# Where tiles begin in SBUF: weights, x and g moved to multiples of 256 bytes in an attention and ReLU-squared feed-forward kernel

## The chip, the cores and the metric

The kernel runs on one core of a Trainium2 chip. The metric is the device time in microseconds of one execution; several executions are timed, and one is profiled.

## The reference

Block-diagonal attention (chunks of 64 positions, no mask), then a feed-forward layer with a squared ReLU, all in float32:

```python
batch, n_heads, seq, head_dim = (8, 8, 576, 64)      # q, k, v
n_tokens, d_model, d_ff = (4608, 512, 2048)          # w_in, w_out

scores = scale * np.matmul(q_c, k_c.transpose(0, 1, 2, 4, 3))   # per chunk of 64
scores = scores - np.max(scores, axis=-1, keepdims=True)
attn = np.exp(scores)
attn = attn / (np.sum(attn, axis=-1, keepdims=True) + 1e-09)
out = np.matmul(attn, v_c)
...
x = out.transpose(0, 2, 1, 3).reshape(B * S, H * D)
h = x @ w_in
r = np.maximum(h, 0.0)
g = r * r
return (g @ w_out).astype(np.float32)
```

The weights arrive as 64-bit floats and are handed to the kernel as pairs of 32-bit words.

## The kernel before

The 4608 tokens are 36 pairs of chunks (128 tokens each), in 9 blocks of 4 pairs. A block's attention output is kept transposed as `xh` and `xl`, a high part in fp32r and the rest, so that a product of float32 quality comes from three fp32r matmuls (high by high, high by low, low by high). The feed-forward part walks over 9 blocks x 16 slices of 128 hidden units. In a slice, L514 makes `h` (128 hidden units x 512 tokens) from 4 x 3 matmuls, in which a piece of `wi` is the resident operand and x moves. ScalarE and VectorE make g = relu(h) squared and split it into `gh` and `gl` (L525 to L541). Two slices later L551 adds 4 x 3 matmuls into four accumulators `o`; there gh or gl is resident and `wo` moves. So each of the 144 slices has 24 matmuls of 128x128 by 512 columns, 3456 in all, each with a weight load of its own.

In the first 120 us the weights come in: `fetch_w` (L126) loads a slice of 64-bit words, and `convert_w` (L137) turns them into float32 and splits them into a high and a low part with ScalarE and VectorE (L147 to L186). Beside that the attention of the first 8 pairs runs. The attention of the other 28 pairs (class `Quad`, L262) is spread between the groups of the feed-forward matmuls, from about 125 to 805 us. TensorE is kept warm in the beginning by matmuls of `ident` with itself (L741, L370).

The order of the instructions on each engine comes from a planner (class `Plan`), which gets a cost in microseconds, the names read and the names written for each step and runs a list schedule; addresses play no part in it.

SBUF is given out by pools in the order in which they are opened: `const` (ident, warm, and 32 slots of 4096 bytes per partition for the weights, some of which hold raw q, k, v first), `att` (row maxima and sums, four buffers of 32 bytes), `xp` (x of two blocks), `gp` (g, gh, gl and the output's staging tile ob), `raw`, `wst`, and `nat`, whose room `late` takes over. Within a pool, tiles follow each other in the order of their first use and take multiples of 32 bytes. Before, the first bytes per partition are:

| tile | begins at | beyond a multiple of 256 |
|---|---|---|
| ident | 16512 | 128 |
| warm | 17024 | 128 |
| first slot of the weights | 17056 | 160 |
| row maxima and sums | 148128 | 160, 192, 224, 0 |
| xh of even blocks | 148256 | 32 |
| g | 181024 | 32 |
| ob | 191264 | 32 |
| raw q and k of the later pairs | 195360 | 32 |
| nat, late | 205600 | 32 |

All tiles in and behind the weights' slots are multiples of 2048 bytes, but for the row maxima and sums, so the rest given for the first of a pool holds for all of it.

Of the kernel before, what the change touches and what calls it, by code (L numbers as in the profile page):

```python
# [10 lines left out]
F32 = mybir.dt.float32  # L11
# [9 lines left out]
def kernel(  # L21
# [24 lines left out]
    P = 128  # L46
# [27 lines left out]
    const = ctx.enter_context(tc.tile_pool(name="const", bufs=1))  # L74
    att = ctx.enter_context(tc.tile_pool(name="att", bufs=1))
# [4 lines left out]
        x: ctx.enter_context(tc.tile_pool(name=f"ps_{x}", bufs=1, space=bass.MemoryType.PSUM))  # L80
        for x in ("o", "h", "at")
    }
    turn_at = itertools.count()

    both = psum["at"].tile([P, 2, DM], F32, name="both", tag="both")
# [4 lines left out]
    early = ctx.enter_context(ExitStack())  # L90

    ident = const.tile([P, P], F32, name="ident")
    warm = const.tile([P, 1], F32, name="warm")


    nat = early.enter_context(tc.tile_pool(name="nat", bufs=1))
# [920 lines left out]
```

## Time and profile before

| | |
|---|---|
| runs | 911.04 us, median of 3 (909.97 to 911.22) |
| profiled execution | 911.28 us, of which the span from the first to the last instruction is 909.5 us |
| mean granted clock of TensorE | 0.997 |
| TensorE matmul, weight load, VectorE, ScalarE busy | 897.6, 724.9, 427.1, 329.9 us |
| HBM read, written | 45.09 MB, 9.44 MB |

In the rows of the profile, PE is TensorE's matmul side and PEld its weight loads, DVE is VectorE, ACT ScalarE, POOL GpSimd and SP the engine that issues most DMAs. A group's row gives the line, the engine, the operation, `out<-in` by tile names, the shape, the count, then busy time in us and the mean of one in ns, then the engine's idle time just before them and what ended it. A row of the chain in order of time or of the timeline begins with the start and the length in us. A row of a tile's view gives the least, median and greatest duration in ns. A row of waits gives microseconds in total, times, and the longest.

### The profile page before, as it was taken

To read this page: it belongs to the slowest core of one execution; us is meant where nothing else is said; L and a number is where in the kernel's file an instruction comes from. 1 tells how busy PE (TensorE), PEld (TensorE's weight loads), DVE (VectorE), ACT (ScalarE), POOL (GpSimd) and SP (SyncE) were. 2 spreads that over 40 slices of the span, in tenths; PEclk is the share of its full clock that TensorE was granted. 3 is DMA by queue.
4 is the path that set the end of the run, shared out by engine and by line. 5 is a ranking of instruction groups with operands and counts; after the bars stand their busy time and mean duration, and the time that the engine had idled before them with its cause. 6 is when DMAs were issued, how large, how long until landed. Compare 5 with 4: busy or idle time off the path is not lost.

```text
span 909.5 us, 14995 instructions
## 1 busy us (share of the span) xinstructions
PE 897.6 (99%) x6046; PEld 724.9 (80%) x6046; DVE 427.1 (47%) x746; ACT 329.9 (36%) x565; POOL 6.1 (1%) x12
## 2 busy tenths in 40 slices
PE   8899999999999999999999999999999999999998
PEld 7677777888888888888888888888888888878886
DVE  5999992333444445444443343444444443223222
ACT  4798873334322223222322222223222322222221
POOL 2000000000000000000000000000000000000000
PEclk9999999999999999999999999999999999999999
DMA  9876533222222223111311131123222210001001
GB/s 196 261 210 177 168 65 97 36 48 46 70 48 36 35 35 83 32 33 31 79 33 32 33 81 29 33 35 81 36 36 36 51 42 1 1 1 47 1 1 46
DMA packets 193237, 55.52 MB, mean 61 GB/s; under 512 B 178192, under 2 KB 186640, under 8 KB 193168
## 3 DMA queue, kind: packets, MB, share of 16 engines
q1 hardware_dynamic: 190912, 53.91, 25.7%
q8 instruction: 47, 0.77, 0.4%
q10 hardware_dynamic: 2256, 0.66, 0.3%
q14 instruction: 22, 0.18, 0.1%
HBM read 45.09 MB, written 9.44 MB: 60 GB/s over the span
## 4 chain that ended last, share of the span: by engine, by line
PE 90%; DVE 5%; ACT 3%; issue 1%; POOL 0%; POOLq 0%; ACTq 0%; DVEq 0%
PE h L514 41%; PE o L551 41%; PE both L331 2%; PE both L291 1%; PE pt L321 1%; DVE gl L541 1%; PE both L741 1%; DVE wia L172 0%; ACT qbd L413 0%; DVE wi L186 0%; DVE wia L165 0%; DVE woa L165 0%; PE sc L425 0%; ACT wi L177 0%; DVE woa L172 0%
## 5 line engine op out<-in xcount | busy, mean ns | idle before, releaser
L514 PE MATMUL h<-xh,wi 128*128 128x512 f32 x1152 | 393.4, 398 | 0.1
L551 PE MATMUL o<-wo,gh 128*128 128x512 f32 x1152 | 361.7, 395 | 0.4 <-ACT ob L565 0.4
L514 PEld LDWEIGHTS h<-xh,wi 128*128 128x128 f32 x1152 | 216.1, 188 | 52.2 <-DVE wi L186 0.5
L551 PEld LDWEIGHTS o<-wo,gh 128*128 128x128 f32 x1152 | 215.8, 188 | 50.8 <-ACT ob L565 0.9
L551 PE MATMUL o<-wo,gl 128*128 128x512 f32 x576 | 227.0, 394 | 0.0
L514 PE MATMUL h<-xl,wi 128*128 128x512 f32 x576 | 226.0, 393 | 0.0
L541 DVE TENSOR_TENSOR gl<-g,gh 128x512 fp32r<-128x512 f32 x144 | 99.3, 690 | 207.3 <-ACT gh L538 204.2
L538 ACT CAST gh<-g 128x512 fp32r<-128x512 f32 x144 | 89.4, 621 | 225.7 <-PE o L551 188.4
L525 ACT ACTIVATE g<-h 128x512 f32<-128x512 f32 x144 | 85.6, 594 | 228.8 <-PE h L514 226.5
L529 DVE TENSOR_TENSOR g<-g 128x512 f32<-128x512 f32 x112 | 76.4, 682 | 184.9 <-ACT g L525 184.9
L551 PEld LDWEIGHTS o<-wo,gl 128*128 128x128 f32 x576 | 108.1, 188 | 25.7
L514 PEld LDWEIGHTS h<-xl,wi 128*128 128x128 f32 x576 | 108.5, 188 | 24.0
L297 DVE TENSOR_REDUCE m<-both 128x8 f32<-128x512 f32 x28 | 19.3, 691 | 55.9 <-ACT xh L341 51.8
L307 ACT ACTIVATE e<-e 128x512 f32<-128x512 f32 x28 | 17.7, 632 | 49.6 <-DVE e L301 49.6
L327 ACT COPY p<-pt 128x512 f32<-128x512 f32 x28 | 16.4, 585 | 20.4 <-PE pt L321 20.4
L341 ACT CAST xh<-both 128x512 fp32r<-128x512 f32 x28 | 16.4, 587 | 14.4 <-PE both L291 13.4
L531 ACT ACTIVATE g<-g 128x512 f32<-128x512 f32 x32 | 20.3, 635 | 0.6
L343 DVE TENSOR_TENSOR xl<-both,xh 128x512 fp32r<-128x512 f32 x28 | 19.1, 681 | 2.1 <-ACT xh L341 2.1
L277 DVE STREAM_TRANSPOSE qt<-q_raw 128x512 f32<-128x512 f32 x28 | 19.6, 700 | 0.0
L331 PEld LDWEIGHTS both<-p,v_raw 64*64 64x64 f32 x896 | 15.6, 134 | 4.9 <-issue 4.9
L331 PE MATMUL both<-p,v_raw 64*64 64x64 f32 x896 | 19.4, 224 | 0.0
L316 DVE TENSOR_TENSOR e<-e,z 128x512 f32<-128x512 f32 x28 | 19.2, 685 | 0.1
(85 smaller groups left out, 461.6 us busy)
## 6 DMA issues: line engine op xcount, KB each, us to landing
wiraw<-in_moe_w_in_dram SPq DMA_DIRECT2D x16, 512.0 KB, 6.6
woraw<-in_moe_w_out_dram SPq DMA_DIRECT2D x16, 512.0 KB, 5.8
out_dram<-ob SPq DMA_DIRECT2D x32, 256.0 KB, 2.0
q_raw<-in_q_dram SPq DMA_DIRECT2D x224, 32.0 KB, 2.2
k_raw<-in_k_dram SPq DMA_DIRECT2D x224, 32.0 KB, 2.2
v_raw<-in_v_dram SPq DMA_DIRECT2D x56, 128.0 KB, 3.3
vbd<-in_v_dram SPq DMA_DIRECT2D x32, 64.0 KB, 3.3
qk_raw<-in_q_dram SPq DMA_DIRECT2D x14, 128.0 KB, 4.8
```

The lines of the kernel that those rows point to most:

```text
L277: nc.vector.transpose(t.rearrange("p h i -> p (h i)"), pairs[self.pair][nm].rearrange("p h a d -> p (h a d)"))
L297: nc.vector.tensor_reduce(self.m, four[:, :, 0], axis=AX.X, op=ALU.max)
L316: nc.vector.tensor_tensor(self.e, self.e, self.z.broadcast_to([P, HH, 2, CH]), op=ALU.mult)
L331: nc.tensor.matmul(four[to, c, 1, h2], self.v[own, 2 * h2 + w], self.p[own, h2, w], start=True, stop=True)
L343: nc.vector.tensor_tensor(xl, four[:, :, 1], xh.bitcast(F32), op=ALU.subtract)
L514: nc.tensor.matmul(self.h[:, :self.n], a[:, c], bb[:, c, :self.n], start=c == 0 and i == 0, stop=last,)
L525: nc.scalar.activation(self.g, self.h[:, :self.n], AF.Relu)
L529: nc.vector.tensor_tensor(self.g, self.g, self.g, op=ALU.mult)
L531: nc.scalar.activation(self.g, self.g, AF.Square)
L538: nc.scalar.copy(self.gh[:, :self.n], self.g)
L541: nc.vector.tensor_tensor(self.gl[:, :self.n], self.g, self.gh.bitcast(F32)[:, :self.n], op=ALU.subtract)
L551: nc.tensor.matmul(acc[b, j], a[:, j * P:(j + 1) * P], bb, start=f == 0 and i == 0, stop=f == NF - 1 and i == 2,)
```

## The change

An unused tile of 128 bytes per partition is put into `att`, and the tile `warm`, of which one column is used, gets 32 columns (128 bytes) in place of one. Nothing else is edited.

```diff
@@ -80,6 +80,7 @@
         x: ctx.enter_context(tc.tile_pool(name=f"ps_{x}", bufs=1, space=bass.MemoryType.PSUM))
         for x in ("o", "h", "at")
     }
+    att.tile([P, 32], F32, name="edge")
     turn_at = itertools.count()
 
     both = psum["at"].tile([P, 2, DM], F32, name="both", tag="both")
@@ -90,7 +91,7 @@
     early = ctx.enter_context(ExitStack())
 
     ident = const.tile([P, P], F32, name="ident")
-    warm = const.tile([P, 1], F32, name="warm")
+    warm = const.tile([P, 32], F32, name="warm")[:, :1]
 
 
     nat = early.enter_context(tc.tile_pool(name="nat", bufs=1))
```

## Prediction, made before the changed kernel ran

> **What bounds the kernel now.** I read the page's head, then its chain that ended last, then the stages, then who waits for whom.
>
> ```profile
> span 909.5 us, 14995 instructions
> PE 897.6 (99%) x6046; PEld 724.9 (80%) x6046; DVE 427.1 (47%) x746; ACT 329.9 (36%) x565; POOL 6.1 (1%) x12
> ...
> PE 90%; DVE 5%; ACT 3%; issue 1%; POOL 0%; POOLq 0%; ACTq 0%; DVEq 0%
> ...
> L514 PE MATMUL h<-xh,wi 128*128 128x512 f32 x1152 | 393.4, 398 | 0.1
> L551 PE MATMUL o<-wo,gh 128*128 128x512 f32 x1152 | 361.7, 395 | 0.4 <-ACT ob L565 0.4
> ...
> L551 PE MATMUL o<-wo,gl 128*128 128x512 f32 x576 | 227.0, 394 | 0.0
> L514 PE MATMUL h<-xl,wi 128*128 128x512 f32 x576 | 226.0, 393 | 0.0
> ```
>
> The last four lines are the 3456 matmuls of the feed-forward part: two lines of 1152 and two of 576. TensorE is 90% of the chain and, before these lines, it waits for somebody for half a microsecond in all. The mean of 393 to 398 ns is the time that one is in flight; they overlap. What one really costs is read from the chain in order of time, where twelve of them stand together.
>
> ```profile
> 265.69 2.78 PE h L514 x12
> ...
> 777.83 2.78 PE o L551 x12
> ...
> 844.11 2.80 PE h L514 x12
> 846.91 2.80 PE o L551 x12
> ```
>
> So one costs 2.78/12 = 231.7 ns in the middle and 2.80/12 = 233.3 ns towards the end, and 3456 of them about 3456 x 0.232 = 802 us of the span of 909.5. The two lines read quite different operands (x moving against a resident w; w moving against a resident g) and cost the same. Next the stages: busy time of each engine, its count, the granted clock and the DMA share.
>
> ```profile
> 0.00:10.00 10.00, 8.65 (x72) 6.93 (x73) 1.54 (x3) 2.07 (x3) 6.05 (x12) 1.00 0.98 180
> 10.00:60.00 50.00, 45.99 (x474) 37.23 (x474) 48.18 (x96) 40.51 (x74) 0.00 (x0) 0.97 0.88 238
> 60.00:120.00 60.00, 57.72 (x438) 45.12 (x433) 57.49 (x113) 50.72 (x92) 0.00 (x0) 1.00 0.56 167
> 120.00:230.00 110.00, 109.58 (x717) 87.89 (x719) 48.98 (x89) 48.17 (x82) 0.00 (x0) 1.00 0.28 53
> 230.00:800.00 570.00, 570.00 (x3880) 463.16 (x3881) 242.50 (x408) 163.48 (x274) 0.00 (x0) 1.00 0.20 42
> 800.00:910.00 110.00, 105.65 (x482) 84.56 (x480) 28.36 (x41) 24.91 (x42) 0.00 (x0) 0.99 0.05 20
> ```
>
> The columns after the length are PE, PEld, DVE, ACT, POOL. In the first 10 us the DMA engines are full (0.98); from 10 to 120 us VectorE is (48.18 of 50, then 57.49 of 60: it converts weights); from 120 us on TensorE is, without a gap from 230 to 800. Three limits in turn, and an address can touch each of them in another way.
>
> **What the change does.** It adds no instruction and takes none away: one tile that nothing writes or reads (128 bytes in each partition), and 128 bytes in place of 32 for `warm`. In the program's address map of before, ident begins at 16512 and ends at 17024, warm takes 32 bytes, and the weights' slots begin at 17056 = 66 x 256 + 160. There are 32 slots of 4096 bytes, then four 32-byte buffers of `att` up to 148256 = 579 x 256 + 32, where x begins; x, g, ob, the raw tiles and the tiles of the attention are multiples of 2048 bytes behind it. So before, each weight begins 160 beyond a multiple of 256 and everything from x on 32 beyond one. Afterwards warm ends at 17152 = 67 x 256, and `att` at 17152 + 131072 + 256 = 148480 = 580 x 256: the weights move up by 96 bytes, all behind them by 224. That it does what it says is therefore settled, except for ident, which stays at 128 beyond. The planner that orders the instructions knows costs and names, not addresses, so the order on every queue stays. There is no new wait, and nothing is moved past anything. What is left is the price of an address, engine by engine.
>
> **TensorE.** Is a moving operand that begins on a multiple of 64 cheaper than one that begins 32 beyond? The one operand of that kind before is ident, at 16512 = 258 x 64. It moves in the transposes and in the warming matmuls; the whole of a run of them and one's time in flight:
>
> ```profile
> 301.34 0.60 PE L321 MATMUL pt<-ident,e 128*128 128x128 f32 x4
> ...
> 32.43 1.05 PE L370 MATMUL h<-ident 128*128 128x256 bf16 x8
> ...
> L321 PE MATMUL pt<-ident,e x112: 270/272/273, 159.4 to 781.5; 128*128 128x128 f32 x112
> ...
> L370 PE MATMUL h<-ident x8: 272/273/283, 32.4 to 33.2; 128*128 128x256 bf16 x8
> ```
>
> Eight bf16 matmuls of 256 columns start within 1.05 - 0.27 = 0.78 us, so one takes 0.78/7 = 111 ns, or 222 ns for 512 columns. The float32 transposes cost (0.60 - 0.27)/3 = 109 ns for 128 columns. So with an operand on a multiple of 64, 512 columns of bf16 stand at 222 ns and 512 columns of the kernel's type, not on one, at 231.7. The 10 ns between them are the most that I can lay at the door of the address: an estimate of 3456 x 9.7 ns = 34 us, 877 us, is the far end below. But the two rows differ in type as well, and the weight loads say that the type alone does such things:
>
> ```profile
> L321 PEld LDWEIGHTS pt<-ident,e x112: 138/141/142, 159.2 to 781.4; 128*128 128x128 f32 x112
> ...
> L551 PEld LDWEIGHTS o<-wo,gh x1152: 186/188/193, 43.1 to 904.8; 128*128 128x128 f32 x192
> ```
>
> e and gh both begin 32 beyond a multiple of 256, both loads have 128 columns of 4 bytes, and one takes 141 ns and the other 188. The kernel's own type (fp32r) costs 47 ns more with the same alignment. That is the nearest row to the question, and by it I put the 10 ns down to the type too and cost the change at nothing on TensorE. The far end above: 2.78 becomes 2.80 wherever it stands, (2.80 - 2.78)/12 = 1.7 ns for each matmul.
>
> **VectorE and ScalarE.** If wide operands off the boundary cost them a piece more, it would show as a rate below one column per step.
>
> ```profile
> L565 ACT COPY ob<-o 128x512 f32<-128x512 f32 x16 | 9.4, 585 | 4.5 <-DMA out_dram<-ob 3.8
> ...
> L565 ACT COPY ob_last<-o 128x256 f32<-128x256 f32 x2 | 0.6, 375 | 0.8 <-PE o L551 0.8
> ...
> L297 DVE TENSOR_REDUCE m<-both 128x8 f32<-128x512 f32 x28 | 19.3, 691 | 55.9 <-ACT xh L341 51.8
> ...
> L529 DVE TENSOR_TENSOR g<-g 128x512 f32<-128x512 f32 x112 | 76.4, 682 | 184.9 <-ACT g L525 184.9
> ```
>
> ScalarE pays (585 - 375)/256 = 0.82 ns a column, with a fixed part of 585 - 420 = 165 ns. VectorE takes 691 ns where it reads 512 columns of PSUM, which the change does not move, and writes 8, and 682 ns where it reads and writes 512 columns of an SBUF tile that begins 32 beyond. The unaligned access is the quicker by 9 ns. So nothing is to be had there: 0. From 120 us on it would be hidden anyway, since VectorE is busy 242.5 of 570 us.
>
> **The DMAs.** Who waits for them:
>
> ```profile
> DVE ob L565 <- DMA out_dram<-ob: 6.3, 8, 2.1
> ...
> ACT kt L417 <- DMA qk_raw<-in_k_dram: 5.4, 1, 5.4
> ...
> ACT ob L565 <- DMA out_dram<-ob: 3.8, 7, 2.1
> ...
> PE o L551 <- ACT ob L565: 0.4, 1, 0.4
> ```
>
> The stores hold up evictions for 10.1 us in all, and of that 0.4 us comes through to TensorE. The one wait for a load is ScalarE's in the first 8 us. After that the loads run ahead of VectorE, whose whole idle time from 10 to 120 us is 110 - 48.2 - 57.5 = 4.3 us: no quicker load can give more than those 4.3 us plus a few tenths ahead of 10 us. On the other side 0: a descriptor that crosses fewer boundaries has no reason to be slower. I take 0, since VectorE keeps its 105.7 us of work in that stage whatever lands sooner.
>
> The page "DMA: Bandwidth & Descriptors" of the Trainium skill says, in "How a descriptor splits into AXI transactions", that a transaction must start at a multiple of 256 bytes, and that the bytes below an unaligned start are fetched and cost beats. It speaks for a gain here. By it a stored row of 2048 bytes, 32 beyond, would take 9 transactions and 65 beats in place of 8 and 64: an estimate of 1.6% of a store, 0.03 us of the 2.0 us in the row below, once at the end of the kernel. No view of this trace shows a transaction.
>
> ```profile
> out_dram<-ob SPq DMA_DIRECT2D x32, 256.0 KB, 2.0
> ```
>
> **The sum** is 0 + 0 + 0 against the profiled execution's 911.28 us (span 909.5 and 1.8 around it); the median of the three runs is 911.04, 0.24 below it, and their spread 909.97 to 911.22 is 0.14%. I predict 911.0. A shift under 0.2%, 1.8 us, can't be told from none.
>
> **The rivals.**
>
> 1. *TensorE reads an aligned row quicker.* For it: the 10 ns over the bf16 rate that nothing else in the trace explains for certain. Against it: the type differs too, and costs 47 ns in the loads at equal alignment. The time: any value down to 877; each nanosecond is 3.5 us.
> 2. *The start gets shorter* (loads that no longer straddle a boundary, or VectorE). For it: a DMA share of 0.98, then 0.88, in the first 60 us. Against it: VectorE is the limit from 10 us on, and its rate shows no loss. At most 911.0 - 4.3 = 906.7.
> 3. *Slower: TensorE falls into the other rhythm.* Without the attention's matmuls between them (844 us) groups take 2.80, with them 2.78, though code, shapes and alignment are the same; so the spacing hangs on something finer than the instructions. Now w and x both begin at 0 within 256 bytes, in place of 160 and 32, and both are read at once. Were that enough for 2.80 everywhere, its place is the stage from 230 to 800 us:
>
> ```profile
> 230.00:800.00 570.00, 287.03 (x1144) 213.34 (x1145) 1.00 0.20 42
> ...
> 230.00:800.00 570.00, 279.77 (x1140) 214.37 (x1140) 1.00 0.20 42
> ```
>
> (first L514, then L551 alone): 2284 matmuls x 1.7 ns = 3.8 us, 914.8. It decides when half of them change. The other way about, 2.78 throughout, gives the 887 or so matmuls after 120 us and outside this stage 1.5 us, which stays within 0.2%.
>
> **How the numbers follow.** No change: 0.60. Rival 1: 0.18, with a third of it at gains under 9 us. Rival 2: 0.07, of which 0.01 stays within 0.2%. Rival 3: 0.15, of which 0.01 stays within it and 0.04 lies beyond 916, should the two reads cost each other more than the other rhythm does. So faster 0.18 + 0.06 = 0.24, same 0.60 + 0.02 = 0.62, slower 0.14. The range of 902 to 916 holds the forecast, rivals 2 and 3 and the small end of rival 1: 0.60 + 0.07 + 0.11 + 0.06 = 0.84.
>
> **What would show it.** Right: twelve matmuls at 2.78 in the middle and 2.80 at the end, LDWEIGHTS of gh at 188 ns, L529 at 682, L538 at its old duration, the loads' landing times unchanged, and VectorE at 48 of 50 us from 10 to 60. Rival 1: groups of twelve below 2.75 us, all through. Rival 2: the same groups, but the first matmul of L514 earlier and a lower DMA share ahead of 60 us. Rival 3: 2.80 from 230 to 800. I am wrong if the price of a matmul hangs on where its rows begin; since 802 us are made of them, nothing else here could move the time by a per cent.

## The result: 911.04 us becomes 894.43 us, and nearly all of it is in the feed-forward matmuls

The changed kernel takes 894.43 us (median of four, 893.91 to 895.09) against 911.04 us (909.97 to 911.22). The ratio is 0.982, with a 95% interval of 0.9803 to 0.9837: 16.6 us, or 1.8%, faster. It lies below the range forecast, and the likeliest case, no change, did not come about.

The changed kernel's lines are one number higher than before's (L515 is L514, L552 is L551). First the head of its page, two of the four lines of the feed-forward matmuls and the one VectorE line that the forecast named:

```profile
span 893.3 us, 14995 instructions
PE 880.5 (99%) x6046; PEld 724.0 (81%) x6046; DVE 427.1 (48%) x746; ACT 330.4 (37%) x565; POOL 6.1 (1%) x12
...
L515 PE MATMUL h<-xh,wi 128*128 128x512 f32 x1152 | 388.1, 394 | 0.2
L552 PE MATMUL o<-wo,gh 128*128 128x512 f32 x1152 | 356.1, 390 | 0.5 <-ACT ob L566 0.5
...
L530 DVE TENSOR_TENSOR g<-g 128x512 f32<-128x512 f32 x112 | 76.4, 682 | 176.1 <-ACT g L526 176.1
```

The instructions are as many as before on each engine. VectorE is busy 427.1 us both times and L530 takes 682 ns as it did; ScalarE's busy time moves by 0.5 us. TensorE's matmul side is 17.1 us less busy, and its weight loads are not (724.0 against 724.9). The chain in order of time gives the price:

```profile
265.15 2.72 PE o L552 x12
...
840.53 2.72 PE h L515 x12
843.25 2.72 PE o L552 x12
```

Twelve take 2.72 us on both lines, in the middle and near the end: 226.7 ns each, against 231.7 and 233.3 before. The two rhythms of before are gone too. When this builds up is read from the first instruction that takes h out of PSUM in a slice: the first slice and the last from the view of the tile g, the sixteenth after it from the timeline; before, then the changed kernel.

```profile
L525 ACT ACTIVATE g<-h x144: 575/597/612, 36.3 to 897.3; 128x512 f32<-128x512 f32 x144
...
140.75 0.60 ACT L525 ACTIVATE g<-h 128x512 f32<-128x512 f32 x1 [2.35 <-PE h L514]
```

```profile
L526 ACT ACTIVATE g<-h x144: 577/598/605, 35.8 to 881.4; 128x512 f32<-128x512 f32 x144
...
139.97 0.60 ACT L526 ACTIVATE g<-h 128x512 f32<-128x512 f32 x1 [2.27 <-PE h L515]
```

The lead is 0.5 us at the first slice, 0.8 at the seventeenth and 15.9 at the last. Between the first two VectorE is the limit, and cheaper matmuls wait for it. In the 127 slices after that, 15.1 us come from 127 x 24 = 3048 matmuls: 5.0 ns each, the difference that the chain shows. So rival 1 is what happened, at about half its far end. But its mechanism, an aligned row that is cheaper to read, is not what the runs below show.

### The profile page after: what moved, and what is told of

It is laid out like the page before. It is cut to its first block, busy times and chain, and to the rows that moved or that the text cites. A ratio compares the mean times of both kernels' runs of the same rounds, so it can differ in the third digit from the quotient of the medians.

```text
span 893.3 us, 14995 instructions
## 1 busy us (share of the span) xinstructions
PE 880.5 (99%) x6046; PEld 724.0 (81%) x6046; DVE 427.1 (48%) x746; ACT 330.4 (37%) x565; POOL 6.1 (1%) x12
## 4 chain that ended last, share of the span: by engine, by line
PE 88%; DVE 5%; DMA 2%; ACT 2%; issue 1%; SPq 1%; POOL 0%; DVEq 0%; POOLq 0%; ACTq 0%
PE h L515 40%; PE o L552 40%; PE both L332 2%; PE both L292 2%; PE pt L322 1%; DMA k_raw<-in_k_dram 1%; DMA woraw<-in_moe_w_out_dram 1%; DMA qk_raw<-in_k_dram 1%; DVE woa L166 1%; PE both L742 1%; PE sc L426 1%; DVE wi L187 1%; DVE wia L173 0%; DVE woa L173 0%; DVE wia L166 0%
## 5 line engine op out<-in xcount | busy, mean ns | idle before, releaser
L515 PE MATMUL h<-xh,wi 128*128 128x512 f32 x1152 | 388.1, 394 | 0.2
L552 PE MATMUL o<-wo,gh 128*128 128x512 f32 x1152 | 356.1, 390 | 0.5 <-ACT ob L566 0.5
L515 PEld LDWEIGHTS h<-xh,wi 128*128 128x128 f32 x1152 | 216.0, 188 | 47.3 <-ACT wi L178 0.6
L552 PEld LDWEIGHTS o<-wo,gh 128*128 128x128 f32 x1152 | 215.4, 188 | 45.6 <-ACT ob L566 0.9
L552 PE MATMUL o<-wo,gl 128*128 128x512 f32 x576 | 224.2, 389 | 0.0
L515 PE MATMUL h<-xl,wi 128*128 128x512 f32 x576 | 223.8, 389 | 0.0
L530 DVE TENSOR_TENSOR g<-g 128x512 f32<-128x512 f32 x112 | 76.4, 682 | 176.1 <-ACT g L526 176.1
L552 PEld LDWEIGHTS o<-wo,gl 128*128 128x128 f32 x576 | 108.1, 188 | 22.7
L515 PEld LDWEIGHTS h<-xl,wi 128*128 128x128 f32 x576 | 108.2, 188 | 21.4
```

The costliest lines, as they stand in the source:

```text
L515: nc.tensor.matmul(self.h[:, :self.n], a[:, c], bb[:, c, :self.n], start=c == 0 and i == 0, stop=last,)
L530: nc.vector.tensor_tensor(self.g, self.g, self.g, op=ALU.mult)
L552: nc.tensor.matmul(acc[b, j], a[:, j * P:(j + 1) * P], bb, start=f == 0 and i == 0, stop=f == NF - 1 and i == 2,)
```

## Experiments

### Which operand: weights alone, x and g alone, and two other common places

Four versions with other sizes of the same two tiles. In the feed-forward part one of the two families (w on one side; x, g, gh and gl on the other) always moves while the other is resident.

```diff
-    att.tile([P, 32], F32, name="edge")
+    att.tile([P, EDGE], F32, name="edge")
...
-    warm = const.tile([P, 32], F32, name="warm")[:, :1]
+    warm = const.tile([P, WARM], F32, name="warm")[:, :1]
```

| version | WARM, EDGE | w begins, mod 256 | x and g begin, mod 256 | median us | ratio to before, 95% interval |
|---|---|---|---|---|---|
| w_alone | 32, 40 | 0 | 32 | 913.63 | 1.0031 (1.002 to 1.0042) |
| x_alone | 8, 56 | 160 | 0 | 915.05 | 1.0045 (1.0029 to 1.0061) |
| both_64 | 48, 32 | 64 | 64 | 894.41 | 0.9821 (0.9805 to 0.9837) |
| both_32 | 40, 32 | 32 | 32 | 895.29 | 0.9829 (0.9813 to 0.9844) |

> Weights on multiples of 256 bytes, x, g and all behind them still 32 beyond one. Moving theory (a matmul costs more when its moving rows begin inside a 64-byte piece; the resident operand's address is free): groups of twelve of L552, where wo moves, take 2.72 us and those of L515, where x moves, keep 2.78 to 2.80; with half of the 15 us gained, 903 us. Resident theory (the weight load is what got cheaper): L515, where wi is resident, takes 2.72 and L552, where gh and gl are, keeps 2.78 to 2.80; also 903 us, so the lines tell these two apart and not the time. Relative theory (what counts is that both operands begin at the same place within 256 bytes): both lines keep 2.78 or more, 911 us. The first loads of q and k go to the weights' slots, so the 0.5 us gained ahead of 36 us should be here if it is theirs.

> x, g and all behind them on multiples of 256 bytes, weights still 160 beyond one. Moving theory: L515 takes 2.72 us for twelve, L552 2.78 to 2.80, 903 us. Resident theory: the other way about, 903 us. Relative theory: both 2.78 or more, 911 us. The start: first relu at 36.3 us as before, if the 0.5 us came from the weights' slots.

> Weights and x, g and all behind them begin 64 beyond a multiple of 256. If 64 bytes are the unit, 2.72 us for twelve on both lines and 894 us, as with 256. If it takes multiples of 128 or 256, 2.78 or more and about 911 us.

> Weights and x, g and all behind them begin 32 beyond a multiple of 256, all at the same place. Moving and resident theory: nothing gained against before, 2.78 to 2.80 for twelve and 911 us. Relative theory: 2.72 and 894 us.

The chain in order of time of w_alone, and then of both_32:

```profile
262.64 2.80 PE o L552 x12
265.45 2.80 PE h L515 x12
```

```profile
262.75 2.72 PE h L515 x12
265.47 2.72 PE o L552 x12
```

With the weights alone on multiples of 256, both lines take 2.80 us and the kernel is 0.3% slower than before. In x_alone, which loses 0.4%, nearly all groups take 2.79 to 2.81 us. With everything 32 beyond a multiple, nearly the whole gain is there. So neither operand's own alignment counts, the moving and the resident theory both fall, and what is left is that the two begin at the same place within 256 bytes. Before, they stood 160 and 32 beyond: apart by 128 on both lines.

### The two lines taken apart, and another distance

Two versions put something between the tiles of one side, so that only one of the two lines keeps operands that agree; the third makes the distance 256 bytes longer. In the first two the lines are numbered two higher than in the changed kernel (L517, L554).

```diff
 # g_off: gh and gl 32 beyond, w and x at 0;   x_off: x 32 beyond, w, gh and gl at 0
+    gp.tile([P, 8], F32, name="gap", bufs=1)             # g_off
+    gp.tile([P, 56], F32, name="gap", bufs=1)            # x_off, with EDGE 40
 # more_between: EDGE 96
```

> The changed kernel with 32 bytes more ahead of g, gh and gl: weights and x stay on multiples of 256, gh and gl (and all behind them) are 32 beyond one. Pair theory (a matmul is dear when its moving operand and the resident operand loaded beside it don't begin at the same place within 256 bytes): L515, whose pair is x and wi, stays at 2.72 us for twelve, and L552, whose pair is wo and gh or gl, goes to 2.80; 894.4 + 1728 x 6.7 ns = 906 us, or less by what the cheap groups between them put back. If the two lines don't come apart (a whole stretch takes one rhythm), both at 2.80 and 914 us.

> The mirror of it: x alone 32 beyond a multiple of 256, weights, g, gh and gl on one. Pair theory: L515 2.80 us for twelve, L552 2.72, 906 us. One rhythm for all: 2.80 on both, 914 us.

> The changed kernel with 256 bytes more between the weights and x: both on multiples of 256, their distance from 131328 to 131584 bytes. If the rule is agreement within 256 bytes, 2.72 us on both lines and 894.4 us. If it was that one distance, 2.78 or more and 911 us.

g_off takes 905.30 us (ratio 0.9943, 0.9926 to 0.9959), x_off 908.62 (0.9978, 0.9969 to 0.9987), more_between 894.89 (0.9831, 0.9817 to 0.9846). The chain of g_off, then of x_off:

```profile
839.59 2.73 PE h L517 x12
842.32 2.79 PE o L554 x12
```

```profile
839.18 2.76 PE o L554 x12
841.94 2.80 PE h L517 x12
```

In g_off the line with agreeing operands (L517: x moves, w is resident) takes 2.73 us and the other 2.79, as the pair theory said. In x_off the order turns round: L517 is dear at 2.80. There L554 reaches 2.76 and not 2.72, and x_off is 2.6 us above the 906 expected. Why the agreeing line keeps half of the loss here and next to none in g_off (2.73) isn't shown. The distance in more_between is another multiple of 256 and has the same 2.72 us:

```profile
262.96 2.72 PE h L515 x12
265.68 2.72 PE o L552 x12
```

### The differences measured by themselves

micro leaves attention and feed-forward out and runs groups of 24 matmuls between two tiles that begin on multiples of 4096.

```python
r = ro // 4 + (x % 3) * step                             # step is 0 in the groups shown
nc.tensor.matmul(o[:, :cols], rs[:, r:r + P], mv[:, mo // 4:mo // 4 + cols], ...)   # x 24
```

> Attention and feed-forward are left out: the kernel loads a piece of q, fills two tiles of 8192 bytes per partition that begin on multiples of 4096, and runs groups of 24 matmuls of 128x128 by 512 columns in fp32r, each with its weight load. A group m<a>r<b> moves columns from byte a of one tile and has the resident operand at byte b of the other. Relative theory with 256 bytes as the unit: 24 matmuls take 5.44 us (226.7 ns each) where b - a is a multiple of 256, whatever a is, and 5.56 to 5.61 us for every other difference of 32 bytes and up. With 64 or 128 bytes as the unit, also where the difference is a multiple of that (against it: before, the difference is 128, and a matmul takes 231.7 to 233.3 ns). Window theory (two reads at one pace that fall on the same part of the memory or not): several neighbouring differences are cheap and the others dear. Moving and resident theory, which the last four runs speak against: cheap for a a multiple of 64, or b. Differences of 4, 8 and 16 bytes: dear by the relative theory if the start itself must agree, cheap if a 32-byte piece is the grain. With 256 and 384 columns the extra over the cheap case is the same 5 to 7 ns if it is paid once for each load, half of it and three quarters if it grows with the columns.

Its chain in order of time (one execution, granted clock 1.00): start, length, and m<moving byte>r<resident byte>n<columns>.

```profile
28.34 5.45 PE m0r0n512b L45 x24
33.79 5.59 PE m0r32n512b L45 x24
...
50.59 5.60 PE m0r128n512b L45 x24
...
61.80 5.51 PE m0r192n512b L45 x24
67.31 5.59 PE m0r224n512b L45 x24
72.90 5.45 PE m0r256n512b L45 x24
...
183.61 5.48 PE m32r32n512b L45 x24
...
211.29 5.47 PE m128r128n512b L45 x24
216.75 5.59 PE m128r256n512b L45 x24
...
227.79 5.59 PE m16r16n512b L45 x24
...
244.35 2.88 PE m0r0n256b L45 x24
247.23 2.84 PE m0r32n256b L45 x24
...
258.62 4.17 PE m0r0n384b L45 x24
262.79 4.16 PE m0r32n384b L45 x24
...
271.14 4.22 PE m0r128n384b L45 x24
```

Here nothing else runs, and the same two prices appear: 5.45/24 = 227 ns where the difference is a multiple of 256, with the moving operand at 0, 32 or 128 (m32r32 and m128r128 take 5.48 and 5.47), and 5.59 to 5.61 us (233 to 234 ns) at the other multiples of 32 from 0 to 544 with the moving operand at 0. The exceptions are 192 and 448 (both 192 beyond), in between at 5.51. The window theory falls: the neighbours 32 to either side of a cheap difference are dear.

Off the multiples of 32 the rule doesn't hold. With both operands at byte 16 the 24 matmuls take 5.59 us, although the difference is 0, and with 16 and 272 they take 5.52; with 16 and 4 (12 short) and with 0 and 240 (16 short) they are cheap, at 5.45 and 5.44. All tiles of the kernel begin on multiples of 32, so this doesn't touch it.

At 384 columns the difference of 32 costs nothing and one of 128 costs 0.05 us in 24 (4.17 and 4.22); at 256 the difference of 32 even gains 0.04. So the loss is neither a fixed price for each load nor one in proportion to the columns. Three resident pieces in turn, 512 bytes apart, behave like one (5.49, 5.59 and 5.57 us at differences of 0, 32 and 128).

micro_two, run once like micro, asks what a group's predecessor does, where between 384 and 512 columns the loss begins, and what bf16 does.

> Again only groups of 24 matmuls between two tiles, attention and feed-forward left out. r<b>after<c>: the resident operand at byte b, moving at 0, after a group with c. If a difference has one price whatever ran before it, r16 and r272 agree in both orders, as do r192 and r128; if a rhythm once found is kept, r16 and r272 are cheap (5.44 us) after r0 and dear (5.59) after r32. By columns at r0, r32, r128: the cheap case takes columns plus 32 cycles (448: 200 ns, 480: 213 ns) and the dear ones come apart from it only somewhere between 384 and 512 columns if what they disturb is the next load's time; at 448 they are already 4 to 6 ns dearer if the loss grows with the columns. bf16 with 512 columns: the same split at multiples of 256 if it is a matter of addresses alone, none if the half as many bytes leave room; then about 216 to 222 ns for all.

```profile
33.14 5.60 PE r16after32x L56 x24
...
55.41 5.60 PE r272after32x L56 x24
...
77.69 5.57 PE r128after32x L56 x24
...
83.26 5.44 PE r0after128x L56 x24
88.70 5.44 PE r16after0x L56 x24
...
110.46 5.44 PE r272after0x L56 x24
...
143.33 5.59 PE r32after0x L56 x24
...
154.37 4.87 PE m0r0n448b L56 x24
159.23 4.91 PE m0r32n448b L56 x24
...
222.79 5.18 PE bf16r32b L49 x24
...
233.15 5.18 PE bf16r128b L49 x24
...
243.51 5.18 PE bf16r256b L49 x24
```

A difference of 16 bytes has no price of its own: it keeps the rhythm that it finds, 5.44 after an agreeing group and 5.60 after one that disagrees, and so does 272. A difference of 32 is dear even after a cheap group. At 128, the difference of before, two dear rhythms appear here too: 5.57 after a group at 32, 5.59 after one at 0. They are close to twice the 2.78 and 2.80 of before; what switches between them isn't shown.

At 448 columns the loss is 0.03 to 0.04 us in 24 (under 2 ns each), 0.05 at 480 and 0.06 to 0.07 at 496, against 0.15 at 512. The cheap case was expected to take the columns plus a fixed part, and near 512 it doesn't: 504 columns take 5.47 us with operands that agree, no less than 512. At 504 a difference of 32 costs 0.04 and one of 128 costs 0.13. bf16 with 512 columns takes 5.18/24 = 216 ns at 32, 128 and 256 alike: there the place is free. Why isn't shown; a bf16 matmul reads half the bytes, and its weight load takes 98 ns in place of 188.

micro_three asks which resident operand has to agree: a matmul's own, or the next one's, which is loaded while it runs. Each pattern runs twice in its one execution, as a and as b.

```python
m, r = moves[x % len(moves)] // 4, stays[x % len(stays)] // 4
# own: moves (0, 32), stays (0, 32)    next: moves (0, 32), stays (32, 0)
```

> Groups of 24 matmuls between two tiles again, attention and feed-forward left out; now the places change from matmul to matmul, to see which two operands have to agree. In own the moving operand alternates between byte 0 and 32 and each matmul's own resident operand begins where its moving one does, so that the next resident operand, loaded while it runs, does not. In next it is the other way: a matmul's own resident operand disagrees, the next one agrees. Theory of the load alongside (what collides is the read of the columns that move with the load of the next resident operand): next 5.44 us, own 5.60. Theory of the matmul's own pair: own 5.44, next 5.60. ownwide, nextwide (0 and 96) and ownthree, nextthree (three places in turn) the same way. same 5.44, none 5.60 as before. half (every second resident operand 32 beyond) and third (every third) say whether each disagreement pays for itself: 5.52 and 5.49 us if it does, 5.60 if one in a few is enough.

```profile
28.86 5.58 PE owna L45 x24
34.44 5.52 PE nexta L45 x24
39.96 5.45 PE samea L45 x24
45.41 5.63 PE halfa L45 x24
51.04 5.59 PE thirda L45 x24
56.63 5.62 PE ownwidea L45 x24
...
67.76 5.59 PE nonea L45 x24
```

Agreement of a matmul's own pair is worth next to nothing (5.58, and 5.62 in the wide variant, against 5.59 for none). Agreement with the next one's load takes about half of the loss away (5.52, and 5.54 the second time; 5.52 in the wide variant, 5.50 with three places). own and next move the same rows in the same order and differ only in which load runs beside which, so the load alongside is a part of the cause. Neither theory gave 5.52, and the other half isn't explained: in next the places also change from matmul to matmul, and each own pair disagrees. Disagreements don't pay one by one: one in three (third) costs as much as disagreement throughout, and one in two (half) costs more, 5.63.

## Why the prediction was wrong

**The step that failed** is the price of an address on TensorE, taken as 0. I had the 10 ns by which an fp32r matmul exceeds the bf16 rate, and put all of it down to the type, because two weight loads with the same alignment differ by type. In truth the address has a share: in micro_two bf16 is at 216 ns (I had read 222 from eight warming matmuls of 256 columns), fp32r with agreeing operands at 226.7, and before was at 231.7 and 233.3. So some 11 ns are the type's and 5 to 7 the address's. The row that I called the nearest was the wrong kind of row. A weight load's duration can't show what its read does to the matmul that runs beside it; LDWEIGHTS of gh stayed at its median of 188 ns in the changed kernel:

```profile
L552 PEld LDWEIGHTS o<-wo,gh x1152: 186/188/192, 42.6 to 888.7; 128*128 128x128 f32 x192
```

**Each operand was looked at alone.** The forecast asked whether a row beginning 32 beyond is dear. both_32 answers no: 895.29 us with every operand 32 beyond. The pair came up in rival 3, with the sign turned round: I feared that operands at the same place would hinder each other, and it is the same place that is cheap. The forecast noted that the two lines cost the same and passed over that their operands stood equally far apart, by 128. The page "TensorE: Matmul & The Clock Gate" of the Trainium skill says in "Step-by-step: what each phase is for" that TensorE has two independent read ports and "Loading the next tile's weights doesn't steal SBUF read bandwidth from the running matmul." For bf16 the runs agree: 216 ns at each of the differences tried. For fp32r with 512 columns they don't: 5.45 or 5.60 us for 24, by the difference of two addresses, with the loads as many and as long, and 5.52 or 5.58 by which load runs beside which matmul (next and own).

**What was right.** Three points. VectorE and ScalarE: 0, as L530's 682 ns shows. The order of the instructions: the 6046 matmuls follow each other by tile names as before. The first 120 us: bound by VectorE, so that even the cheaper matmuls gained only 0.3 us between the first and the seventeenth slice.

**The DMAs** were near enough in the time (the first slice leads by 0.5 us) and wrong in the detail that nothing changes there. The stage from 0 to 10 us, with the DMA share and GB/s in the last two columns, of both_32 (the weights' slots, into which the first q and k go, 32 beyond) and of w_alone (on a multiple of 256):

```profile
0.00:10.00 10.00, 8.64 (x73) 6.86 (x74) 1.58 (x3) 2.07 (x3) 6.06 (x12) 1.00 0.99 178
```

```profile
0.00:10.00 10.00, 8.64 (x76) 6.84 (x77) 1.98 (x3) 2.07 (x3) 6.06 (x12) 1.00 0.88 197
```

Five kernels with those slots on multiples of 256 move 197 to 206 GB/s there, four without 178 to 183. This goes the way of rival 2, and of the Trainium skill's page "DMA: Bandwidth & Descriptors" ("How a descriptor splits into AXI transactions"), although that page speaks of the side that is read and these transfers write to SBUF. No run shows a transaction. What the quicker loads are worth isn't shown either: against before, the first slice starts 0.7 us earlier in w_alone and not at all earlier in more_between, whose loads are as quick, and 2.0 us earlier in both_64, whose loads are among the slow ones (its granted clock from 10 to 60 us was 1.00, against 0.97 in the other eight).

**What stays open** is the mechanism within the memory. The runs show the condition (the difference of the two addresses, modulo 256), the place (fp32r, near 512 columns) and the part of the load alongside. Why 192 lies in between, why a 16-byte difference keeps whatever rhythm it finds, and what decides off the multiples of 32, they don't show.

## What to carry to other kernels

Where every matmul has its own weight load, the type is fp32r and the moving operand is 512 columns wide, let the two families of operands begin at the same place modulo 256 bytes, on a multiple of 32; which of those tried (0, 32, 64, 128) made next to no difference, and aligning one of the families alone can lose time (913.63 and 915.05 us). The difference of two addresses is a property of the whole allocation: a small tile put between two pools was worth 1.8% here. When a price is to be read from a trace, look for a row in which the same two things run side by side, not for one of each alone.

## What the hardware showed that was not expected

- An fp32r matmul of 128x128 by 512 columns with its own weight load takes 226.7 ns when its operands begin on multiples of 32 and agree modulo 256, and 231.7 to 234 ns when they don't (229.6 at 192 beyond), while the load itself stays at 188 ns. With both at byte 16 it takes 233 ns, although they agree.
- The loss depends on the width: at a difference of 32, 0.14 us in 24 matmuls at 512 columns, 0.04 at 448 and none at 384; at 128 still 0.05 at 384. For bf16 there is none at 512.
- There is a memory of the rhythm: at a difference of 16 bytes the same 24 matmuls take 5.44 or 5.60 us, depending on the group that ran before.
- The first transfers of q and k ran at 197 to 206 GB/s into slots on multiples of 256 bytes, and at 178 to 183 GB/s into others.
